# Local attention and channel mix: narrow products from unit 5, a halved first magnitude, new orders

## The chip, the cores and the metric

The kernel runs on one core of a Trainium2 chip. The metric is the device time of one execution in microseconds; the kernel before took 376.92 us (median of three runs, 376.2 to 378.92).

## What is computed

Sequences of 768 tokens, 4 of them, 8 heads of 64. Queries in chunks of 32 see 16 keys to the left, their own 32, 8 to the right and 8 memory keys: 64 keys, where the sequence has them all. The result, token by token 512 wide, goes through a channel mix with the token before it.

```python
def _attn_ref(q, k, v, mem_k, mem_v):
    ...
    for c in range(nc):
        ...
        k_full = np.concatenate([mem_k, k_ctx], axis=2)
        v_full = np.concatenate([mem_v, v_ctx], axis=2)
        scores = scale * np.matmul(q_c, k_full.transpose(0, 1, 3, 2))
        scores = scores - np.max(scores, axis=-1, keepdims=True)
        a = np.exp(scores)
        a = a / (np.sum(a, axis=-1, keepdims=True) + 1e-09)
        out[:, :, c_start:c_end] = np.matmul(a, v_full)

def _moe_ref(x, mu_k, mu_r, w_k, w_v, w_r):
    x_prev = np.concatenate([np.zeros((B, 1, D), dtype=np.float32), x[:, :-1, :]], axis=1)
    xk = mu_k * x + (1.0 - mu_k) * x_prev
    xr = mu_r * x + (1.0 - mu_r) * x_prev
    k = np.maximum(xk @ w_k, 0.0)
    v = k * k @ w_v
    r = 1.0 / (1.0 + np.exp(-(xr @ w_r)))
    return (r * v).astype(np.float32)
```

## The kernel before

The 3072 tokens are 12 **units** of 256 tokens, each of two **tiles** of 128. For each unit TensorE does, in this order of dependence:

- `s`, the scores (tile names s, PSUM, L572), from which VectorE takes the maximum (mx, L585) and subtracts it (L590), ScalarE the exponential (L596), VectorE the sum (L600) and the normalisation (L606). The PSUM buffer of the scores is one, and a narrow product (below) uses the same;
- from unit 3 on (MOVED) a transpose of e by VectorE (eT, L880), written to DRAM (eD) and read back as aTz by four transfers (L891); for units 0 to 2 four TensorE transposes for each tile (`t`, pt, L731), copied to aTz by ScalarE or VectorE (L390);
- `a`, the attention product px from aTz and the values vw. It has two forms. The **wide** one (L751, units 0 to 5) is sixteen 64x2x32 matmuls for each tile and gives the product already turned (64 passes for both tiles); ScalarE copies it to xT. The **narrow** one (L823, from unit ROWX = 6 on) is 64 small matmuls for both tiles (128 passes in the trace); a VectorE transpose of the result (L830) goes to DRAM (xD, L836) and returns as xT by four transfers (L841);
- the token mix (df L957 or L969, then xf, and xr as df, L989 and L991), split in a high part (xh) and a low part (xl, L1012);
- `h0` to `h3`, the projections with w_k (ph, L1459), then the squared relu (kf, ah, al) on ScalarE and VectorE; `g0` and `g1`, the gates with w_r (pr, L1348) of the unit after; `p1` to `p7`, seven Strassen-like products with w_v (accx, accy, accz, L1250), from which VectorE builds the output o (L1289, L1292, L1315 to L1322).

Unit 0 works in whole fp32 (ph L1405, pr L1339, pv L1548), unit 1 in split parts without the Strassen form (ph L1434, pv L1561). Products in split parts take three passes: high by high, low by high, high by low.

A weight chunk of 1 MB is loaded to raw (L438 for w_k, L440 for w_r and w_v), its magnitude is taken by ScalarE (w from raw, L456), its low bits by VectorE (L459), and both are joined by VectorE (L463). w0 to w3 are chunks of w_k, w4 and w5 of w_r, w6 to w9 of w_v; v2 and v3 are the values of tiles 2 and 3, q0a to q5 the queries and keys of units.

The order of TensorE is written by hand: LEAD for units 0 and 1, then STAGES, one line for each unit u, whose names mean: h, p and g as above (g of unit u+1), s the scores of unit u+2 and z those of u+3, a and b the products of the two tiles of unit u+1, x the product of unit u+2. A stage that is not listed takes line 0. LOADS orders the loads of SyncE's queue. The class Plan sets the orders of VectorE, ScalarE and the other transfers: it places each operation by a cost in us, by its due time and by what it depends on, and reckons with pauses in TensorE's instruction fetch (`fetched`). At the start some dependences are added by hand, so that the first unit's work goes in a set order (`prior`). While TensorE waits for its first operands it runs warm-up matmuls on zeros (warm, L1619), whose number is reckoned from the planned waiting time; an instruction of 512 columns is two passes in the trace.

## Time and profile before

| | before |
|---|---|
| timed runs | 376.92 us (376.2 to 378.92) |
| profiled execution | 378.26 us |
| its span | 376.4 us |
| TensorE busy | 369.4 us, 98% |
| TensorE's weight loads | 340.4 us, 90% |
| VectorE busy | 319.4 us, 85% |
| ScalarE busy | 211.1 us, 56% |
| chain that ended last | TensorE 80%, VectorE 13%, transfers 3%, ScalarE 2% |

The share of busy time of an engine tells how full it is on average; the view of waits tells what it stood idle for, and the chain of work follows the end back to its beginning. A matmul's row gives a start and a modelled end, and the next one starts before that end; so what one costs is read from start to start. A row of the timeline with x64 is a run of 64 matmuls of one kind, with the time from the first's start to the last's end. Bracketed at a row's end stands how long the engine was idle ahead of it, and what ended that.

### The profile page before, as it was taken

The numbers are of one execution on the slowest core, as the hardware profiler recorded it, in microseconds if no ns is written. First come the engines' busy times: TensorE is split into PE (matmuls) and PEld (weight loads), VectorE is DVE, ScalarE is ACT, GpSimd is POOL, SyncE is SP. The second block draws the span as 40 slices with busy tenths as digits, with TensorE's granted clock in tenths as the row PEclk, the third lists the DMA queues.
The fourth block names the chain that finished last, engine by engine and source line by source line (L and its number), as shares of the span: only waits on it lengthen the run. The fifth ranks groups of instructions, "written<-read, shape, count | busy, mean of one in ns | idle before, by whom it ended". The sixth has DMA issues, their size and how long they took to land.

```text
span 376.4 us, 11488 instructions
## 1 busy us (share of the span) xinstructions
PE 369.4 (98%) x5086; PEld 340.4 (90%) x5086; DVE 319.4 (85%) x518; ACT 211.1 (56%) x311; POOL 2.4 (1%) x9
## 2 busy tenths in 40 slices
PE   8999999999899999999999999999999999999996
PEld 6786579888899999999999999899999999999996
DVE  3898999899989599889878969998998997779274
ACT  2787897874585287355256447449339254154350
POOL 2000000000000000000000000000000000000000
PEclk9999999999999999999999999999999999999999
DMA  8999963222831743664693276186343431200101
GB/s 311 419 406 407 367 238 128 70 84 103 276 117 57 231 165 113 241 208 173 250 307 117 77 241 246 71 264 227 113 171 115 159 121 63 81 29 0 57 1 57
DMA packets 24146, 64.78 MB, mean 172 GB/s; under 512 B 2720, under 2 KB 10784, under 8 KB 23712
## 3 DMA queue, kind: packets, MB, share of 16 engines
q1 hardware_dynamic: 24096, 64.04, 47.9%
q8 instruction: 40, 0.66, 0.7%
q14 instruction: 10, 0.08, 0.1%
HBM read 49.88 MB, written 14.16 MB: 170 GB/s over the span
## 4 chain that ended last, share of the span: by engine, by line
PE 80%; DVE 13%; DMA 3%; ACT 2%; issue 1%; SPq 0%; DVEq 0%
PE ph L1459 25%; PE pr L1348 11%; PE accy L1250 10%; PE accx L1250 7%; PE accz L1250 6%; PE s L572 4%; PE pv L1561 3%; PE ph L1434 3%; PE px L751 3%; PE ph L1405 3%; PE warm L1619 2%; PE pv L1548 2%; PE px L823 2%; DVE al L1195 2%; DMA xT<-xD 1%
## 5 line engine op out<-in xcount | busy, mean ns | idle before, releaser
L1459 PE MATMUL ph<-xh,wk 128*128 128x256 f32 x320 | 89.0, 278 | 0.0
L1459 PE MATMUL ph<-xl,wk 128*128 128x256 f32 x320 | 88.0, 275 | 0.0
L1459 PE MATMUL ph<-xh,wl 128*128 128x256 f32 x320 | 88.0, 275 | 0.0
L1478 ACT ACTIVATE kf<-ph 128x512 f32<-128x512 f32 x46 | 27.0, 598 | 88.6 <-PE ph L1459 78.4
L1459 PEld LDWEIGHTS ph<-xh,wk 128*128 128x128 f32 x320 | 61.4, 192 | 0.8
L1459 PEld LDWEIGHTS ph<-xh,wl 128*128 128x128 f32 x320 | 61.4, 192 | 0.0
L1459 PEld LDWEIGHTS ph<-xl,wk 128*128 128x128 f32 x320 | 61.4, 192 | 0.0
L390 ACT CAST ah<-kf 128x512 fp32r<-128x512 f32 x47 | 28.7, 622 | 17.1 <-DVE kf L1173 11.6
L1195 DVE TENSOR_TENSOR al<-kf,ah 128x512 fp32r<-128x512 f32 x50 | 33.9, 683 | 2.5 <-ACT ah L390 2.2
L1348 PE MATMUL pr<-wr,xh 128*128 128x512 f32 x88 | 33.6, 382 | 0.0
L1348 PE MATMUL pr<-wl,xh 128*128 128x512 f32 x88 | 33.4, 379 | 0.0
L1348 PE MATMUL pr<-wr,xl 128*128 128x512 f32 x88 | 33.4, 379 | 0.0
L1485 ACT ACTIVATE kf<-kf 128x512 f32<-128x512 f32 x45 | 28.0, 633 | 1.0
L1250 PE MATMUL accx<-wv,ah 128*128 128x256 f32 x80 | 22.4, 280 | 0.0
L1250 PE MATMUL accx<-wl,ah 128*128 128x256 f32 x80 | 22.0, 275 | 0.4 <-issue 0.4
L1250 PE MATMUL accx<-wv,al 128*128 128x256 f32 x80 | 22.0, 275 | 0.0
L596 ACT ACTIVATE e<-e 128x1024 f32<-128x1024 f32 (+1 forms) x12 | 12.3, 1027 | 12.5 <-DVE e L590 12.5
L1357 ACT ACTIVATE sg_sb<-pr 128x512 f32<-128x512 f32 x24 | 14.0, 598 | 9.4 <-PE pr L1348 9.2
L1348 PEld LDWEIGHTS pr<-wr,xl 128*128 128x128 f32 x88 | 16.6, 189 | 2.3
L1348 PEld LDWEIGHTS pr<-wr,xh 128*128 128x128 f32 x88 | 16.7, 190 | 2.0
L1348 PEld LDWEIGHTS pr<-wl,xh 128*128 128x128 f32 x88 | 16.7, 190 | 1.8
L572 PEld LDWEIGHTS s<-qk 64*32 64x32 f32 x1472 | 15.4, 105 | 3.2 <-issue 2.2
(165 smaller groups left out, 964.3 us busy)
## 6 DMA issues: line engine op xcount, KB each, us to landing
qk<-in_qk_dram SPq DMA_DIRECT2D x23, 768.0 KB, 5.8
vw<-in_vw_dram SPq DMA_DIRECT2D x24, 512.0 KB, 5.2
out_dram<-o SPq DMA_DIRECT2D x23, 256.0 KB, 3.0
eD<-eT SPq DMA_DIRECT2D x9, 512.0 KB, 3.0
aTz<-eD SPq DMA_DIRECT2D x36, 128.0 KB, 3.1
raw<-in_w_v_dram SPq DMA_DIRECT2D x4, 1024.0 KB, 10.2
raw<-in_w_k_dram SPq DMA_DIRECT2D x3, 1024.0 KB, 13.0
xD<-aTz SPq DMA_DIRECT2D x6, 512.0 KB, 2.6
```

The costliest lines, as they stand in the source:

```text
L390: e.copy(dst, src)
L572: nc.tensor.matmul(s5[CHUNK * j : CHUNK * (j + 1), h, d - c, r, :], *operands(ts[d], r, j, slice(64 * h, 64 * h + 64)), start=True, stop=True,
L596: nc.scalar.activation(e, e, AF.Exp, scale=SCALE)
L751: nc.tensor.matmul(p3[64 * h : 64 * h + 64, 2 * g : 2 * g + 2, CHUNK * j : CHUNK * j + CHUNK], v[:, g, h, j, :], a[:, h, g, j, :], start=True,
L1195: nc.vector.tensor_sub(low(n), place[n](), T["ah", u, n].bitcast(F32))
L1250: nc.tensor.matmul(o, x, w, start=(n in fresh and c + i == 0), stop=(c == cs[-1] and i == 2), skip_group_check=True)
L1348: nc.tensor.matmul(pairs(p), x[:, place_of(u)[k], c * P : (c + 1) * P], woven(w), start=(k + n == 0), stop=(k == KT - 1 and n == 2),)
L1357: nc.scalar.activation(sg, p, AF.Sigmoid)
L1405: nc.tensor.matmul(p[:, i * UTOK + c * P : i * UTOK + (c + n) * P], T["w", id(wk_hl[0]), k][:, fc], T["xf", u, 0][:, k, z], start=(i + k + ...
L1459: nc.tensor.matmul(pairs(p[:, i * UTOK : (i + 1) * UTOK]), w[:, fc], x[:, :, place_of(u)[k]].rearrange("p t n -> p n t"), start=(k + n == ...
L1478: e.activation(part(), p, AF.Relu)
L1485: e.activation(q, q, AF.Square)
```

## The change

- ROWX falls from 6 to 5: unit 5's product takes the narrow form.
- The magnitude of w0 is taken in two halves of 128x512 (HALF). The sum of the first unit's first tile is done in two parts, the first of them as soon as its exponential is there.
- Of the dependences added by hand at the start two go (FORCE "nec" names those that stay): the copies of tile 1's transposes need no longer be ScalarE's, and w0's magnitude need no longer follow tile 0's copies.
- LOADS: w6, the first chunk of w_v, goes behind w7 and w8, and q5 ahead of q4.
- LEAD and the STAGES of units 2, 3, 4, 5, 9, 10, 11 and of line 0 are new.
- The planner's reckoning of fetch pauses, three of its costs and slacks, and the divisor by which the first group of warm-up matmuls is counted are changed; the first group has three instructions instead of four, the others as many as before.

```diff
-LOADS = "q0a q0b q1 id w0 v0 v1 w1a q2 w1b w2 w3 w4 q3 w5 w6 v2 w7 w8 w9 v3 q4 q5"
-LEAD = "s0.0.0 s0.0.1 s0.1 t0 t1 a0 a1 h0.0.0 h0.0.1 s1.0 h0.1.0 h0.2.0 h0.3.0 s1.1 h0.3.1 h0.3.2 h0.3.3 g0.0.0 g0.1.0 g0.0.1 t2 g0.1.1 t3 a2 v0.0.0 a3 v0.1.0 s2.0 v0.1.1 h1.0.0 h1.0.1 h1.0.2 v0.0.1 h1.0.3 h1.1.0 h1.1.1 h1.1.2 t4 t5 h1.1.3 a4 v1.0.0 a5 g1.0 g1.1 v1.0.1 s3.0 g2.0 v1.1.0 g2.1 v1.1.1"
+FORCE = "nec"
+HALF = 2
+LOADS = "q0a q0b q1 id w0 v0 v1 w1a q2 w1b w2 w3 w4 q3 w5 w7 w8 w6 v2 w9 v3 q5 q4"
+LEAD = "s0.0.0 s0.0.1 s0.1 t0 t1 a0 a1 h0.0.0 h0.0.1 s1.0 h0.1.0 h0.2.0 h0.3.0 s1.1 h0.3.1 g0.0.0 g0.1.0 h0.3.2 g0.0.1 h0.3.3 t2 t3 g0.1.1 a2 v0.0.0 a3 v0.1.0 s2.0 v0.1.1 v0.0.1 h1.0.0 h1.0.1 h1.0.2 h1.0.3 h1.1.0 h1.1.1 s3.0 t4 h1.1.2 h1.1.3 t5 v1.0.0 a4 a5 g1.0 v1.0.1 g1.1 v1.1.0 g2.0 g2.1 v1.1.1"
...
-    0: "z h0 h1 h2 h3 x p1 g0 p6 p7 g1 p5 p2 p4 p3",
-    2: "s h0 h1 a b h3 h2 p1 p7 g0 p6 g1 p5 p2 p3 p4",
+    0: "h0 h1 h2 z h3 p1 x g0 p6 p7 g1 p4 p5 p2 p3",
+    2: "h0 h1 s h2 a b h3 p1 p7 g0 p2 p6 g1 p5 z p3 p4",
...
-ROWX = 6
+ROWX = 5
...
-        def f_abs(z):
-            if z == 0:
+        def f_abs(z, n=1, h=0):
+            if z + h == 0:
                 T["w", id(hi), k] = sb(f"w{i}", [P, 2 * DM], f"w{i}")
-            m = T["w", id(hi), k][:, cols(z)]
-            nc.scalar.activation(m, word(1, F32, z), AF.Prelu, scale=TINY, alpha=-(2.0**32))
+            c = cols(z)
+            m = (c.stop - c.start) // n
+            m = slice(h * m, (h + 1) * m)
+            nc.scalar.activation(
+                T["w", id(hi), k][:, cols(z)][:, m], word(1, F32, z)[:, m], AF.Prelu, scale=TINY, alpha=-(2.0**32)
+            )
...
-        by = [("act", 0.5)] if t == 1 else either(act=(0.5,), dve=(0.61,))
+        by = [("act", 0.5)] if t == 1 and "t" in FORCE else either(act=(0.5,), dve=(0.61,))
...
-        if t == 0:
+        if t == 0 and "c" in FORCE:
             prior["abs"].deps += [c0, c1]
...
-                n = 0 if ("ph", 0, 0) in T else int((o.start - busy - 0.2) / (0.43 if busy else 0.86))
+                n = 0 if ("ph", 0, 0) in T else int((o.start - busy - 0.2) / (0.43 if busy else 1.1))
```

The orders of the two programs, first ScalarE's queue at the start, from the exponential of the first unit on (aTz are the turned probabilities, w from raw the magnitude of w0, xf the token mix). Before:

```order
L596 ACTIVATE e_137<-e_137 128x2x256
L390 COPY aTz<-pt_205 64x512 x2
L456 ACTIVATE w_229<-raw_187 128x1024
L390 COPY aTz<-pt_220 64x512 x2
L930 ACTIVATE xf_0_251<-px_234,mu_sb 128x128
L390 COPY xT_254<-px_234 128x4x128
L456 ACTIVATE w_274<-raw_198 128x512
```

In the changed kernel, from the same place:

```order
L613 ACTIVATE e_136<-e_136 128x2x256
L466 ACTIVATE w_208<-raw_187 128x512
L398 COPY aTz<-pt_199 64x512 x2
L466 ACTIVATE w_208<-raw_187 128x512
L398 COPY aTz<-pt_222 64x512
L951 ACTIVATE xf_0_251<-px_234,mu_sb 128x128
L398 COPY xT_255<-px_234 128x4x128
```

One half of the magnitude moved ahead of the first copies, the other stays between the copies, and of the second tile's two copies one has left this queue (it stands in VectorE's).

Then VectorE's queue around unit 3's transpose of e (mx, e, sum and eT belong to unit 3; `w` from `w` are sums of weight chunks, xl low parts of the mix). Before:

```order
L1058 TENSOR_TENSOR w_464<-w_496,w_464 128x4x128
L581 MEMSET s_0_994 32x2x4x16
L585 TENSOR_REDUCE mx_0_1063<-s_0_994 128x16
L590 TENSOR_TENSOR e_1080<-s_0_994,mx_0_1063 128x1024
L1012 TENSOR_TENSOR xl_0_1083<-df_945,xh_0_989 128x1024
L1058 TENSOR_TENSOR w_472<-w_526,w_472 128x4x128
L1058 TENSOR_TENSOR w_496<-w_496,w_464 128x4x128
L600 TENSOR_REDUCE sum_0_1087<-e_1080 128x16
L601 TENSOR_SCALAR sum_0_1087<-sum_0_1087 128x16
L602 RECIPROCAL sum_0_1087<-sum_0_1087 128x16
L606 TENSOR_TENSOR e_1080<-e_1080,sum_0_1087 128x1024
L880 STREAM_TRANSPOSE eT_1132<-e_1080 128x1024
```

In the changed kernel:

```order
L607 TENSOR_TENSOR e_1035<-s_0_807,mx_0_997 128x1024
L1607 TENSOR_TENSOR o_0_1037<-pv_0_932,sg_sb 128x512
L1012 SCALAR_TENSOR_TENSOR df_1015<-df_1015,mu_sb,xT_974 128x256 x4
L400 CAST xh_1_1060<-xf_1017 128x1024
L1033 TENSOR_TENSOR xl_1_1062<-xf_1017,xh_1_1060 128x1024
L617 TENSOR_REDUCE sum_0_1091<-e_1035 128x16
L618 TENSOR_SCALAR sum_0_1091<-sum_0_1091 128x16
L619 RECIPROCAL sum_0_1091<-sum_0_1091 128x16
L1033 TENSOR_TENSOR xl_0_1095<-df_1015,xh_0_1058 128x1024
L623 TENSOR_TENSOR e_1035<-e_1035,sum_0_1091 128x1024
L901 STREAM_TRANSPOSE eT_1112<-e_1035 128x1024
L1079 TENSOR_TENSOR w_487<-w_487 128x4x128
```

The sums of weight chunks that stood between the scores and the transpose of e now stand behind it, and a cast of xh with its low part xl_1 stands between.

Last TensorE's queue at unit 5's product. Before, it stands between two groups of projections:

```order
L1459 MATMUL ph_0_2068<-xh_0_1942,wk_71 128x256
L1459 MATMUL ph_0_2068<-xl_0_2015,wk_71 128x256
L1459 MATMUL ph_0_2068<-xh_0_1942,wl_735 128x256
L751 MATMUL px_2101<-aTz,vw_1725 64x2x32 x16
L751 MATMUL px_2124<-aTz,vw_1750 64x2x32 x16
L1459 MATMUL ph_1_2145<-xh_0_1942,wk_68 128x256
L1459 MATMUL ph_1_2145<-xl_0_2015,wk_68 128x256
```

In the changed kernel it stands between two of the seven products with w_v, one stage earlier:

```order
L1271 MATMUL accz_1946<-wv_73,ah_3_1831 128x256
L1271 MATMUL accz_1946<-wl_756,ah_3_1831 128x256
L1271 MATMUL accz_1946<-wv_73,al_3_1822 128x256
L844 MATMUL px_1974<-vw_1730,aTz 32x64 x32
L844 MATMUL px_1974<-vw_1757,aTz 32x64 x32
L1271 MATMUL accy_2046<-mh_1205,ah_3_1926 128x256
L1271 MATMUL accy_2046<-tl,ah_3_1926 128x256
```

The form changed from two groups of sixteen 64x2x32 matmuls to two rows of thirty-two 32x64 ones, whose operands change places, and the place moved from stage 4 into stage 3.

## Rows read from the trace of the kernel before

**Rows 1.** The page: busy times; then granted clock and GB/s in 40 slices.

```profile
PE 369.4 (98%) x5086; PEld 340.4 (90%) x5086; DVE 319.4 (85%) x518; ACT 211.1 (56%) x311; POOL 2.4 (1%) x9
...
PEclk9999999999999999999999999999999999999999
...
GB/s 311 419 406 407 367 238 128 70 84 103 276 117 57 231 165 113 241 208 173 250 307 117 77 241 246 71 264 227 113 171 115 159 121 63 81 29 0 57 1 57
```

**Rows 2.** TensorE's waits: line, releaser, then us, times, longest.

```profile
PE px L751 <- DMA aTz<-eD: 1.0, 1, 1.0
PE px L751 <- ACT aTz L390: 0.7, 1, 0.7
PE accy L1250 <- DVE o L1292: 0.5, 1, 0.5
PE accx L1250 <- issue: 0.4, 1, 0.4
```

**Rows 3.** TensorE's timeline, first 17 us: start, length, what [idle before it].

```profile
1.18 3.78 PE L1619 MATMUL warm<-zero_sb 128*128 128x256 f32 x8 [1.18 <-DVE zero_sb L380]
4.89 1.19 PE L654 MATMUL s<-qk 64*32 64x48 f32 x64
...
8.57 2.42 PE L1619 MATMUL warm<-zero_sb 128*128 128x256 f32 x10
...
15.23 1.15 PE L751 MATMUL px<-aTz,vw 128*64 128x64 f32 x32 [0.67 <-ACT aTz L390]
16.31 0.94 PE L1405 MATMUL ph<-xf,w 128*128 128x128 f32 x6
```

**Rows 4.** ScalarE's timeline from 9 to 17 us.

```profile
11.58 1.17 ACT L390 COPY aTz<-pt 64x512 f32<-64x512 f32 x2 [0.70 <-PE pt L731]
12.78 1.20 ACT L456 ACTIVATE w<-raw 128x1024 f32<-128x1024 f32 x1
...
16.55 0.69 ACT L456 ACTIVATE w<-raw 128x512 f32<-128x512 f32 x1
```

**Rows 5.** The chain that ended last, from 80 to 104 us: start, length, what.

```profile
81.55 1.43 PE s L572 x89
...
87.22 1.20 DVE w L1058 x2
...
97.03 4.44 DMA aTz<-eD
...
101.51 2.09 PE px L751 x64
```

**Rows 6.** TensorE's timeline around unit 5's product.

```profile
157.05 2.08 PE L751 MATMUL px<-aTz,vw 128*64 128x64 f32 x64
159.06 0.38 PE L1459 MATMUL ph<-xh,wk 128*128 128x256 f32 x1
159.28 0.28 PE L1459 MATMUL ph<-xl,wk 128*128 128x256 f32 x1
```

**Rows 7.** TensorE's timeline around unit 6's product.

```profile
176.85 1.48 PE L823 MATMUL px<-vw,aTz 64*32 64x64 f32 x128
178.27 0.38 PE L1250 MATMUL accy<-t1h,ah 128*128 128x256 f32 x1
```

**Rows 8.** VectorE's timeline, one row.

```profile
223.39 1.21 DVE L957 TENSOR_TENSOR df<-xT 128x1008 f32<-128x1008 f32 x1 [3.25 <-DMA xT<-xD]
```

**Rows 9.** The loads of w_v: issue, landing, ScalarE, VectorE and the first reader.

```profile
25.50 9.37 SPq L440 DMA_DIRECT2D raw<-in_w_v_dram  x3
...
raw<-in_w_v_dram SPq DMA_DIRECT2D x4, 1024.0 KB, 10.2
...
36.41 1.16 ACT L456 ACTIVATE w<-raw 128x1024 f32<-128x1024 f32 x1 [0.71 <-DMA raw<-in_w_v_dram]
...
38.48 2.35 DVE L463 SCALAR_TENSOR_TENSOR w<-w,raw 128x1024 uint32<-128x1024 uint32 x2
...
41.84 1.13 PE L1548 MATMUL pv<-w,kf 128*128 128x512 f32 x2
```

## Prediction before the changed kernel was run

> **What bounds the kernel now.** I read the page first, then TensorE's waits, then the chains of the places where it waits. The page's line of busy times says that TensorE works 369.4 us of the 376.4 us span, 98%, while VectorE stands at 85% and ScalarE at 56% [rows 1]. So only two things can shorten the kernel: less work in TensorE's queue, or fewer of its gaps, and there are few of those. The view of TensorE's waits lists what is left to take [rows 2]: an attention product that waited 1.0 us for a transfer (aTz<-eD), one that waited 0.7 us for ScalarE's copies at the start, a partial sum that waited 0.5 us for VectorE, and 0.4 us that the view puts to "issue". With the stretch before the first projection (ph at 16.31 us, [rows 3]) this is all that a new order could win; the rest is matmuls that stand in both kernels.
>
> **The start.** TensorE's timeline shows eight passes of the warm-up matmul, then the first scores at 4.89, and so on to the last attention product at 15.23 and the first ph at 16.31 [rows 3]. Eight passes are four instructions; of the changed program's order the first group has three. They took 3.78 us, 0.47 a pass, so two passes less put the first scores 0.94 us earlier, if their operands are there; the other warm-up groups have the same counts as before. Further down it is ScalarE that decides: its row shows copies at 11.58, then the 1.20 us magnitude of the first weight chunk at 12.78, then the other tile's copies [rows 4], and the product at 15.23 waits for those copies by the view of waits (0.7, [rows 2]). ScalarE had been idle 0.70 us ahead of 11.58. Half a magnitude is the 128x512 form, 0.69 us [rows 4]. Cut in two, the first half fits into that idle 0.70, and one of the later two copies may go to VectorE; what stays between the copies is 0.69 instead of 1.20. That is 0.51 us on the path if all else stays, and the earlier scores add something unless VectorE, serial here, holds them. The cost of the cut is one more instruction, 2 x 0.69 - 1.20 = 0.18 us, which lies in ScalarE's idle time. I take -0.55. Bounds: -0.75 (the whole 0.7 wait, and a little of the 0.94), and +0.3 if the scores run at the slow pass for longer (below).
>
> The passes of the first group take 0.47 us, those of the third 0.24 [rows 3]: the array works at half its pace at first and at its full one later, though the page's line of the granted clock reads nine tenths or more, the 2.4 GHz level, in every slice [rows 1]. The Trainium skill, "TensorE: Matmul & The Clock Gate", section "What's actually happening", says that the throttled state is the default and activity releases it; that would speak against a warm-up matmul less, and the rows agree with the two paces but show no run with another count.
>
> **Unit 5's product, narrow instead of wide.** The wide pair of unit 5 starts at 157.05 and the projection behind it at 159.06: 2.01 us [rows 6]. The narrow form that unit 6 on already uses starts at 176.85 and is followed at 178.27: 1.42 us [rows 7]. Difference -0.59; I take -0.60. Its price lies elsewhere: one VectorE transpose of 1.2 us and a round trip through DRAM of the product. The row of VectorE shows what such a trip can cost: it sat idle 3.25 us until the last xT transfer landed at 223.39 [rows 8]. The product of unit 5 stands a stage ahead of its use, so I count 0 for the trip, and VectorE, busy 85% of the span [rows 1], carries 1.2 us more. If the cover is gone, the mix of unit 5 is late by up to 3 us, and the projections of unit 5 behind it: that would turn the -0.6 into a loss of 2.4.
>
> The narrow form is 64 instructions, 128 passes in the row, in 1.42 us: 22 ns from one instruction to the next [rows 7]. The Trainium skill, "TensorE: Matmul & The Clock Gate", section "Wait — 56ns, not 53.3ns?", says that this distance never falls below about 25 ns however small the matmul; by that (an estimate) the product takes 1.6 us if an instruction is meant, a term of -0.4, and 3.2 us if a pass is, a loss of 1.2. The row shows the very operation at 1.42, below both, so the sum goes by it.
>
> **The order of TensorE.** A small product between projections costs a pass twice its size behind it: the next ph starts 0.22 us after the one that follows the product, where 0.11 is the pitch of a 128x256 pass [rows 6]; the same 0.1 is lost ahead of it. So each place where the array goes from projections to small products and back costs some 0.2 us. I counted these places in both orders: 27 before, 26 in the changed one. Term: -0.2.
>
> **Unit 3's scores earlier.** The largest gap ends at 101.51 (1.0 us, and some 0.1 around it). Its chain reads backwards from the product at 101.51 to the transfer that ran from 97.03 for 4.44 us, past VectorE's sums of weight chunks at 87.22, and to unit 3's scores at 81.55 [rows 5]. From scores to product these are 20 us. The changed order puts these scores behind h1.1.1, ahead of two quarters of a projection, two tiles' transposes and products, two gates and two parts of v1 that stood before them, while the product stays near its place. It is VectorE's queue that passes the gain on. Before, five sums of weight chunks stand ahead of the transpose of e, 0.6 each (two take 1.20, [rows 5]); in the changed order none does, and two casts come in that another engine did before. I reckon these at 0.7 each, as the 128x512 pass of ScalarE (an estimate, from [rows 4]). So the transpose comes 3.0 - 1.4 = 1.6 us earlier, and 1.0 suffices. Term: -1.1 (the wait and the 0.1). Bounds: 0, if VectorE takes its maximum and subtraction no earlier than now, and -1.1. The scores share one PSUM buffer, so those of the next unit wait for their subtraction; that is ready long before.
>
> **The loads.** The first chunk of w_v goes from the first place among its four loads to the third. The issue row of the three later ones starts at 25.50 and ends 9.37 later [rows 9], so the last is issued near 34.5. The second landed at 36.41, since ScalarE waited for it till then; the transfers move some 407 GB/s in that slice [rows 1], 2.6 us for 1 MB. So what comes third lands between 36.4 and 39.0; I take 37.7. Then 1.16 for its magnitude and 1.18 for its join (half of 2.35) [rows 9]: ready at 40.0, at worst 41.3. Its first reader, v0.0.0, starts at 41.84 now, and 0.75 earlier with the start and the switch saved: 41.1. So 0 to 0.2 us of wait. The values of the second tile (v2) land 1.3 us behind, 39.0 (up to 40.3), and the product that reads them is half a wide pair ahead of v0.0.0, at 40.1. I take +0.1 for both.
>
> **Other waits.** Against the sum for accy (VectorE's o, [rows 2]) and the 0.4 of issue the new orders of six stages may do anything: those gaps go or others come. VectorE's queue in the third stage is the tightest place, since unit 3's softmax and mix fall together there with a product's conversions. The nearest rows are the present gaps, 0.5 and 0.4 [rows 2]. I take 0: as much comes as goes. Bounds: -1.0 (none comes) and +1.5 (three more of 0.5).
>
> **The sum.** -0.55 - 0.60 - 0.20 - 1.10 + 0.10 + 0 = -2.35 us. The profiled run took 378.26 us (span 376.4), so 375.9 in its own terms; it stands 1.3 us above the median of the three timed runs, 376.92 (376.2 to 378.92). From the median: 374.6 us, 0.6% less.
>
> **Rivals.**
> - *Everything comes.* Start -0.75, product -0.6, switch -0.2, unit 3's wait -1.1, and both small waits gone, -1.0: -3.65, 373.3 us; with a little more from the scores' 0.94, 1%. For it: each part has its row, and the gaps do not depend on each other. Against: six stages get new orders, and no row shows that these leave no gap.
> - *The waits form again.* Unit 5's conversions and unit 3's softmax meet on VectorE, and +1.5 stands where 0 was: 376.1 us, a gain of 0.2%. For it: VectorE at 85%. Against: it has 57 us idle in all.
> - *The first w_v chunk comes late* (the other side). If its buffer comes free only when the last chunk's does now, it is issued at 34.5, and lands by the median of 10.2 us [rows 9] at 44.7; ready 47.0, 5.9 us behind 41.1, and nothing of the other chunk is ready to fill it: 380.4 us. A landing by 38.8 costs nothing; from 41.2 on, 2.4 us later, the whole gain is eaten and the kernel is slower than before. For it: the row of 9.37 us for three issues is mostly waiting. Against: of these three only the last waits long, if the second was issued near the first, as its landing at 36.41, 10.9 us after 25.50, says.
> - *The array speeds up later*, with a warm-up matmul less: the scores and the warm passes up to 8.57 then run at 0.47 instead of 0.24, at most 0.9 us on the path: 375.5 us.
> - *The narrow product is slow here*, 3.2 us, if each of its passes keeps a distance of its own: +1.8 on the sum, 376.4 us. Unit 6's row of 1.42 speaks against it. (This is what the page's rule above would do.)
>
> **How the numbers follow.** My forecast (between -1.5 and -3.2 us) has 0.54, everything 0.17, waits formed again 0.17, the late chunk 0.08, the late clock 0.03, the slow narrow product 0.01. The range leaves out 2 in 10: below, everything by 0.9 us of the runs' own scatter (376.92 - 376.2 = 0.7, and 0.2 of the scores), 372.4; above, the waits formed again by +1.5 of the scatter (half of the 2.0 between median and highest, and 0.5), 377.6. A measurement of this kernel can tell about 1%, 3.8 us, from no change. Faster by more than that is only the case in which everything comes: 0.17. Slower by more needs 380.7, half of the late chunk's chance: 0.04. The rest, 0.79, lies within 1%.
>
> **What would show it.** In the changed kernel's timeline the first ph should start near 15.75; the list of TensorE's waits should have no px for aTz<-eD near 100; the product of unit 5 should be a row of about 1.42 us; v0.0.0 should follow the product ahead of it without idle time. The prediction is wrong if TensorE's idle time after the first ph is above 3 us or below 1, or if the first ph starts after 16.3.

## The result: 379.6 us against 377.4, and the profile after

Eight executions of the changed kernel have a median of 379.58 us (377.83 to 381.51), eight of the kernel before on the same chip 377.37 us (376.2 to 378.92). The ratio is 1.0065, with a 95% interval of 1.0037 to 1.0092: slower by 0.65%, where 0.6% less was forecast. The profiled execution took 379.40 us, its span is 377.6.

The page of the changed kernel, in four of its lines: the span, the busy times (they answer [rows 1]), the granted clock in 40 slices, and the transfers of instructions in queue q8 with packets, MB and share.

```profile
span 377.6 us, 11611 instructions
...
PE 369.3 (98%) x5148; PEld 339.9 (90%) x5148; DVE 323.0 (86%) x522; ACT 206.6 (55%) x309; POOL 2.4 (1%) x9
...
PEclk9999999999999999999999998999999999999999
...
q8 instruction: 40, 0.66, 0.7%
```

TensorE is as busy as before, 369.3 us, in a span that is 1.2 us longer. One slice of the clock, the 25th, is below nine tenths. TensorE's waits (line, releaser, then us, times, longest; they answer [rows 2]):

```profile
PE px L844 <- issue: 2.0, 1, 2.0
...
PE px L772 <- ACT aTz L398: 0.6, 2, 0.3
PE px L844 <- PE accx L1271: 0.5, 1, 0.5
PE s L671 <- DMA qk<-in_qk_dram: 0.3, 1, 0.3
...
PE px L844 <- DMA aTz<-eD: 0.2, 1, 0.2
```

Unit 3's wait for aTz<-eD of 1.0 us, that for VectorE's o and the 0.4 of "issue" at accx are gone from this list, as hoped. In their place one product, the narrow one of unit 8, has 2.0 us of "issue" in it and 0.5 us ahead of it. TensorE's timeline there (start, length, what, [idle before it]):

```profile
225.19 0.28 PE L1271 MATMUL accx<-wv,al 128*128 128x256 f32 x1
225.95 1.43 PE L844 MATMUL px<-vw,aTz 64*32 64x64 f32 x110 [0.49 <-PE accx L1271]
229.42 0.41 PE L844 MATMUL px<-vw,aTz 64*32 64x64 f32 x18 [2.03 <-issue]
...
230.39 0.63 PE L1369 MATMUL pr<-wr,xl 128*128 128x512 f32 x1
230.82 0.63 PE L1369 MATMUL pr<-wr,xh 128*128 128x512 f32 x1
...
233.92 0.38 PE L1369 MATMUL pr<-wr,xl 128*128 128x512 f32 x1
```

The product starts at 225.95, runs 110 of its 128 passes, and stands still until 229.42 with nothing to wait for: in the trace none of its instructions between 226.05 and 229.42 waits for a semaphore. Behind it the gate's passes start 0.43 us apart (230.39, 230.82) where 0.22 is the rule. The windows around the pause (us, then busy time of PE, PEld, DVE, ACT, POOL with counts, granted clock, DMA share, GB/s) show why:

```profile
226.20:226.90 0.70, 0.70 (x86) 0.70 (x83) 0.70 (x2) 0.56 (x2) 0.00 (x0) 1.00 0.00 0
229.90:231.90 2.00, 2.00 (x6) 1.62 (x7) 2.00 (x2) 1.98 (x2) 0.00 (x0) 0.57 0.56 158
231.90:233.40 1.50, 1.50 (x5) 1.14 (x5) 0.34 (x1) 0.00 (x0) 0.00 (x0) 0.50 0.91 358
```

The granted clock is 1.00 in the product and 0.57 and then 0.50 behind the pause, which is the 1.2 GHz level; the trace's record of the clock has it from 230.18 to 233.60.

The 0.5 us ahead of the product are another thing. The view puts them to accx, whose last matmul had ended at 225.47, but the product writes to the PSUM buffer of the scores, and VectorE's subtraction, which empties this buffer of unit 9's scores, ends at 225.85, 0.10 us before the product starts:

```profile
224.63 1.22 DVE L607 TENSOR_TENSOR e<-s,mx 128x1024 f32<-128x1024 f32 x1
```

The start came out better than forecast in this execution. Its timeline (answers [rows 3]):

```profile
1.18 2.93 PE L1640 MATMUL warm<-zero_sb 128*128 128x256 f32 x6 [1.18 <-DVE zero_sb L388]
4.04 0.68 PE L671 MATMUL s<-qk 64*32 64x48 f32 x32
4.99 0.46 PE L671 MATMUL s<-qk 64*32 64x48 f32 x32 [0.27 <-DMA qk<-in_qk_dram]
5.38 1.56 PE L1640 MATMUL warm<-zero_sb 128*128 128x256 f32 x6
...
13.93 1.15 PE L772 MATMUL px<-aTz,vw 128*64 128x64 f32 x32 [0.31 <-ACT aTz L398]
15.02 2.05 PE L1426 MATMUL ph<-xf,w 128*128 128x128 f32 x16
```

The first ph starts at 15.02, 1.29 us earlier than before. TensorE's last matmul, however, starts at 374.25, where before it was at 372.94. So the way from the first ph to the last matmul, which I call **the stretch** from here on, went from 356.6 to 359.2 us: +2.6, where the sum had -1.8.

### The profile page after: what moved, and what is told of

The parts are those of the page before. It is cut to its first block, busy times and chain, and to the rows that moved or that the text cites. A ratio compares the mean times of both kernels' runs of the same rounds, so it can differ in the third digit from the quotient of the medians.

```text
span 377.6 us, 11611 instructions
## 1 busy us (share of the span) xinstructions
PE 369.3 (98%) x5148; PEld 339.9 (90%) x5148; DVE 323.0 (86%) x522; ACT 206.6 (55%) x309; POOL 2.4 (1%) x9
## 4 chain that ended last, share of the span: by engine, by line
PE 77%; DVE 9%; DMA 9%; ACT 2%; issue 1%; SPq 1%; DVEq 0%
PE ph L1480 25%; PE pr L1369 14%; PE accy L1271 10%; PE accx L1271 6%; PE accz L1271 6%; DMA sg_sb<-in_w_r_dram 4%; PE pv L1582 4%; PE s L589 3%; PE ph L1455 3%; PE px L844 3%; DMA eD<-eT 2%; PE pv L1569 2%; DMA raw<-in_w_k_dram 2%; PE px L772 1%; DVE w L475 1%
## 5 line engine op out<-in xcount | busy, mean ns | idle before, releaser
L1499 ACT ACTIVATE kf<-ph 128x512 f32<-128x512 f32 x47 | 27.8, 597 | 92.4 <-PE ph L1480 91.7
L398 ACT CAST ah<-kf 128x512 fp32r<-128x512 f32 x49 | 29.6, 620 | 16.6 <-DVE kf L1194 13.9
L1369 PE MATMUL pr<-wr,xh 128*128 128x512 f32 x88 | 34.4, 391 | 0.0
L1369 PE MATMUL pr<-wr,xl 128*128 128x512 f32 x88 | 34.2, 389 | 0.0
L1506 ACT ACTIVATE kf<-kf 128x512 f32<-128x512 f32 x47 | 29.3, 631 | 2.4 <-DVE kf L1501 1.2
L1369 PEld LDWEIGHTS pr<-wr,xh 128*128 128x128 f32 x88 | 17.1, 194 | 2.4
L1369 PEld LDWEIGHTS pr<-wl,xh 128*128 128x128 f32 x88 | 17.1, 194 | 2.1
L589 PEld LDWEIGHTS s<-qk 64*32 64x32 f32 x1472 | 15.3, 105 | 2.7 <-issue 1.5
L589 PE MATMUL s<-qk 64*32 64x64 f32 x1472 | 17.4, 225 | 0.0
```

Of the source, the lines that this page charges most:

```text
L398: e.copy(dst, src)
L589: nc.tensor.matmul(s5[CHUNK * j : CHUNK * (j + 1), h, d - c, r, :], *operands(ts[d], r, j, slice(64 * h, 64 * h + 64)), start=True, stop=True,
L1369: nc.tensor.matmul(pairs(p), x[:, place_of(u)[k], c * P : (c + 1) * P], woven(w), start=(k + n == 0), stop=(k == KT - 1 and n == 2),)
L1499: e.activation(part(), p, AF.Relu)
L1506: e.activation(q, q, AF.Square)
```

## The experiments

The question was what the pause inside unit 8's product is, since it and what lies around it hold more than the whole loss: 0.5 us of wait ahead of it, 2.25 of pause and 1.7 of half pace make 4.5 us. (A pause is counted here from one matmul's start to the next one's; the idle time in brackets, from the modelled end, is 0.2 to 0.4 us less.) The experiments come in the order in which they were run. All ratios are to the kernel before, run beside them; "stretch" is read from each trace as above.

**One stage's order put back.**

```diff
+    6: "z h0 h1 h2 h3 x p1 g0 p6 p7 g1 p5 p2 p4 p3",
```

> The changed kernel with one stage's order put back: in stage 6 the scores of unit 9 stand ahead of h0 and unit 8's narrow product behind h3, as before. Theory F (in the changed kernel's stage 6 the scores and the narrow product, 256 PE records each, stand so close together, around a 1.5 MB load of queries, that the instruction fetch comes late inside the product: 2.0 us of 'issue' at 227.4, and then about 1.6 us in which the granted clock is at its lower level): no pause over 0.7 us in stage 6, no lower clock, TensorE's last matmul 3.5 to 4.5 us earlier than in the changed kernel, time near 375.2 (379.6 - 4.4). Rival P (the pause belongs to the place in the program, not to that order): a pause of about 2 us stays near 227 or comes in the next stage, time within 1 us of the changed kernel's.

Measured: 383.93 us, ratio 1.0174 (1.0104 to 1.0244). The pause is there, and longer: the product starts at 224.66 and stands still 2.6 us (2.41 idle) ahead of its last six passes. Another product waits 4.7 us at 261.92, 0.10 us behind the end of VectorE's subtraction at 261.82: the queues were laid out anew, and it waited for the scores' buffer. Theory F as I had put it (too little distance between scores and product) falls: with four groups of projections between them the pause stays. The number of TensorE's instructions ahead of the product is nearly the same in both orders, and this is what led further.

**The product one gate later.**

```diff
+    6: "h0 h1 h2 z h3 p1 g0 x p6 p7 g1 p4 p5 p2 p3",
```

> The changed kernel with unit 8's narrow product one gate later in stage 6 (behind g0 instead of ahead of it), 2.6 us further from unit 9's scores. Theory F: the fetch has 2.6 us more, so the pause of 2.0 us inside the product falls below 0.5 us and the clock stays at its upper level; the 0.5 us wait ahead of the product (for the scores' PSUM buffer) goes too; time near 375.2. Rival P: the pause stays at 1.5 us or more. A cost on the other side: the product's transfers come 2.6 us later, which may show as idle time of VectorE ahead of df, up to 1 us on TensorE.

Measured: 379.21 us, ratio 1.0047 (1.0016 to 1.0078), where 375.2 was forecast. The pause is down to 0.8 us (0.59 idle, where less than 0.5 was forecast), and no lower clock follows it; but the planner laid out other queues anew, and a product a stage earlier waits 2.35 us at 205.16, which takes the gain. The view puts this wait to "issue"; the rows of VectorE and TensorE show that it is the scores' buffer again, since the subtraction ends at 205.06:

```profile
203.84 1.22 DVE L608 TENSOR_TENSOR e<-s,mx 128x1024 f32<-128x1024 f32 x1
205.16 1.14 PE L845 MATMUL px<-vw,aTz 64*32 64x64 f32 x56 [2.35 <-issue]
```

**The loads of queries moved away.**

```diff
+        moved = [o for o in ops if getattr(o, "tile", 0) in (20, 21)]
+        queue = [o for o in ops if o.eng == "dma"]
+        goal = queue[queue.index(moved[-1]) + 7]
+        ops = [o for o in ops if o not in moved]
+        i = ops.index(goal) + 1
+        ops[i:i] = moved
```

> The changed kernel with only one thing moved: the two loads of unit 10's queries and keys (768 KB each), issued at 220.7, are issued behind unit 8's xT transfers (about 238). All engines' orders are the same otherwise. Theory F1 (the instruction fetch was late because it stood behind these loads, which filled the DMA engines from 223 to 226): the pause inside unit 8's product shrinks from 2.0 us to under 0.7 us, no lower clock, time near 375.8. Rival F2 (the fetch is late because 256 records of the product go through in 1.4 us, whatever the DMA engines do): the pause stays at 1.7 to 2.3 us and the time within 1 us of the changed kernel's. Between: about 1 us.

Measured: 379.79 us, ratio 1.006 (1.0035 to 1.0085), as the changed kernel. TensorE's timeline at the product:

```profile
228.37 1.43 PE L845 MATMUL px<-vw,aTz 64*32 64x64 f32 x110 [0.50 <-PE accx L1272]
231.84 0.41 PE L845 MATMUL px<-vw,aTz 64*32 64x64 f32 x18 [2.03 <-issue]
```

The pause has 2.03 us of idle time again and comes behind the 110th pass again, though the DMA engines were idle while the product ran (a share of 0.00 from 228.4 to 229.4). F1 falls: these loads are not the cause.

**The start alone.** The tables of before, with the start of the changed kernel:

```diff
-ROWX = 5
+ROWX = 6
...
```

> The changed kernel with the tables of before put back (order of the loads, LEAD, all STAGES, ROWX = 6), so that of the change only the start (halved magnitude, split sum, the two dependences less, a warm-up instruction less) and the planner's reckoning stay. Theory: the start alone gives 1.2 us, so the first ph begins at 15.0 to 15.2 and the time is 1.0 to 1.5 us under that of before (about 376.0 against 377.4). Rival: the start's gain is given back at the next wait (loads that come no earlier than before hold the first unit's chunks): the first ph at 15.1, but less than 0.4 us left at the end.

Measured: 382.58 us, ratio 1.0131 (1.0084 to 1.0178), stretch 362.6. It does not answer its question: the changed planner lays the old tables out worse (unit 3's product waits 2.5 us at 103.95 for aTz<-eD), and the first ph was at 17.08 though its program at the start is the same. That made the start itself a question.

**What the traces had in common.** Each q8 transfer of the page brings 0.66 MB / 40 = 16.5 KB (16,384 bytes in the trace), and the 10,296 matmuls and weight loads of the changed kernel make 257 for each. So I counted TensorE's instructions (matmuls, weight loads and semaphore instructions of the trace) up to each pause that no operand and no buffer explains:

```
kernel                       record at which it pauses   record mod 256   from the transfer's start to the end of the pause
before                       5824                        192              2.57 us
changed                      6848                        192              2.41 us
one stage's order put back   6848                        192              2.42 us
product one gate later       6848                        192              2.20 us
loads moved away             3776, 6848                  192              2.43, 2.42 us
start alone                  5824, 8128                  192              2.18, 2.36 us
```

The pauses stand 256 records apart or a multiple of it, and end 2.2 to 2.6 us after a q8 transfer begins. If that is the cause, a pause must move when instructions are put ahead of everything, whatever the order behind them.

**56 records more, order unchanged.** The 14 warm-up matmuls cut in two (the same for four in the two runs behind it). Each of them has 256 columns, not the 512 that the section on the kernel before gives, and leaves two weight loads and two matmuls in the trace, so each cut adds four records:

```diff
+PIECES = [2] * 14
...
+                    n = 2 * P // PIECES[0]
+                    for x in range(PIECES.pop(0)):
+                        nc.tensor.matmul(warm[:, x * n : (x + 1) * n], zero_sb[:, :P], zero_sb[:, x * n : (x + 1) * n], start=True, stop=True)
```

> The changed kernel with each of the 14 warm-up matmuls of 256 columns cut into two of 128: the same work and the same orders of all engines, but 56 PE records more ahead of everything. In all traces so far pauses inside a stream of PE instructions stand at record 256k+192 of the trace, and end 2.4 us after an instruction transfer begins. Theory A (the pause of 2.2 us inside unit 8's product, and the lower clock behind it, come from where the boundary of a 256-instruction block falls): with the boundary 56 records earlier in the program, the block that ends inside the product has some 3 us of slow projections in it; the pause at the product's 110th matmul goes or falls under 0.8 us, no pr at half pace behind it, and the stretch from the first ph to the last matmul shrinks from 359.2 us to about 355 to 356.5. A pause may come up at another burst, at record 256k+192 again. Rival B (the product waits for data in its middle): the pause stays at the 110th matmul, 2.0 to 2.4 us.

Measured: 381.64 us, ratio 1.0126 (1.0108 to 1.0144). Unit 8's product runs through. Pauses stand at records 3264, 5056 and 7872, all 192 mod 256, the last two in the middle of projections and of a gate that run behind narrow bursts:

```profile
168.27 0.28 PE L1481 MATMUL ph<-xl,wk 128*128 128x256 f32 x1
170.38 0.27 PE L1481 MATMUL ph<-xh,wl 128*128 128x256 f32 x1 [1.83 <-issue]
...
258.75 0.38 PE L1370 MATMUL pr<-wr,xl 128*128 128x512 f32 x1
260.98 0.38 PE L1370 MATMUL pr<-wr,xh 128*128 128x512 f32 x1 [1.85 <-issue]
```

Theory A holds for where the pause is, and B falls. Its size I had wrong: the stretch is 359.3, since 0.6 + 2.1 + 2.2 us of pauses came in the place of the one, where 355 to 356.5 was forecast. The clock stayed at 1.00 in this trace.

**112 and 168 records more.**

> As the run before, but 112 PE records more (seven warm-up matmuls cut in four, seven in two). Theory A: the pause is not at the 110th matmul of unit 8's product; where pauses inside a stream are, they stand at record 256k+192; the stretch from first ph to last matmul is 354.5 to 357.5, by the luck of the other bursts. Rival B: the same pause at the same place as in the changed kernel, stretch near 359.

> As the two runs before, but 168 PE records more (all warm-up matmuls cut in four). Theory A: as for 112 records; boundaries fall 168 records earlier in the program, so bursts that were safe may be hit and the reverse; pauses only at record 256k+192. Rival B: unchanged pause.

Measured: 397.87 and 400.5 us, ratios 1.0548 (1.0503 to 1.0592) and 1.062 (1.0605 to 1.0636). Most of that is the start: in these two the first ph comes at 25.6 and 33.1 us, because passes of 64 columns start 0.213 us apart like those of 128, and the pace is slow through most of the head (in the second, four transposes at 28.5 take 1.06 us where 0.60 is the rule). Behind it the pauses are at records 4288, 5056, 7872 and at 4288, 8896, once more all 192 mod 256, between 1.2 and 4.2 us long, and unit 8's product runs through in both (having waited 0.5 and 1.0 us for the scores' buffer). So theory A holds for the place. Its stretch for the first of the two, 354.5 to 357.5, missed: it is 365.1 us, with three pauses of 1.6 to 3.2 us and two spells at the lower clock; in the second it is 362.1.

**Four warm-up instructions.**

```diff
-                n = 0 if ("ph", 0, 0) in T else int((o.start - busy - 0.2) / (0.43 if busy else 1.1))
+                n = 0 if ("ph", 0, 0) in T else int((o.start - busy - 0.2) / (0.43 if busy else 0.86))
```

> The changed kernel with four instructions instead of three in the first warm-up group, as before. In five traces of kernels with three the first ph starts at 15.0, 15.2, 16.3, 17.0 and 17.1 us, since the warm-up and score passes change from 0.47 to 0.24 us at anything from 5.9 to 9.9 us; PE idles 0.2 to 0.3 us ahead of the second half of the first scores. Theory W (the missing warm-up matmul leaves that idle time, and the pace then sometimes rises later): with four the idle time is gone, the pace changes by 7 us and the first ph starts at 15.3 to 15.9 here. Rival V (the moment varies from run to run with three or four): the pace changes at 8 us or later in this run too, or the idle time is gone without effect. The rest as in the changed kernel, with the pause in unit 8's product (four records' shift).

Measured: 379.35 us, ratio 1.0049 (1.0014 to 1.0084), with the pause at record 6848. The idle time ahead of the second half of the scores is gone, the trace's record of the faster clock begins at 7.40, and the first ph is at 16.23. Theory W's time for it was too early by 0.3, but its main point (the faster pace comes near 7 us) is borne out. The median is the same as with three.

**The gate ahead of the product, nothing else.** If the block that ends inside the product had more slow work in it, the transfer would be there in time. One swap of two neighbours in TensorE's order, all other queues kept:

```diff
+        gate = [o for o in ops if o.eng == "pe" and o.rank == due["g", 7, 0]]
+        product = [o for o in ops if o.eng == "pe" and o.rank == due["a", 16]]
+        ops = [o for o in ops if o not in gate]
+        i = ops.index(product[0])
+        ops[i:i] = gate
```

> The changed kernel with one swap in TensorE's order: in stage 6 the gate g0 stands ahead of unit 8's narrow product instead of behind it; the orders of all other engines are the same. Theory A (instruction blocks of 256 records): the block in which the product ends now has 24 slow gate records more ahead of it, so the pause inside the product falls from 2.25 us to 0.5 to 1.0 us; the wait of 0.6 us for the scores' buffer ahead of it goes; no pr runs at half pace behind it (1.6 us). The stretch from first ph to last matmul falls from 359.2 us to 355.2 to 356.0, the time to 375.5 to 376.5, against 377.4 before. Rival D (the gain is given back because the product, 2.6 us later, delays unit 8's mix): stretch 357.5 or more, with idle time of TensorE behind VectorE's df of unit 8.

Measured: 375.72 us (374.39 to 376.74, 12 runs), ratio 0.9936 (0.9914 to 0.9959). The whole list of TensorE's waits in this kernel, and its timeline at the product:

```profile
PE warm L1646 <- DVE zero_sb L388: 1.2, 1, 1.2
PE px L772 <- ACT aTz L398: 0.6, 2, 0.3
PE s L671 <- DMA qk<-in_qk_dram: 0.3, 1, 0.3
PE ph L1426 <- DVE xf L959: 0.2, 1, 0.2
```

```profile
229.10 0.38 PE L1369 MATMUL pr<-wr,xl 128*128 128x512 f32 x1
229.41 1.48 PE L844 MATMUL px<-vw,aTz 64*32 64x64 f32 x128
230.82 0.38 PE L1271 MATMUL accy<-mh,ah 128*128 128x256 f32 x1
```

The product follows the gate without a pause and takes 1.41 us; there is no "issue" left. The trace shows how close this is. The transfer that brings the next block begins at 227.72, now 1.69 us ahead of the product and not 1.05 behind its start, and record 6848 is reached at 230.35, 2.63 us after the transfer began; the pauses end 2.2 to 2.6 us after one. The wait for the scores' buffer is gone too, since the subtraction had ended at 227.28. The stretch is 354.0 us, 5.2 less than in the changed kernel: more than forecast, since even the 0.5 to 1.0 us that I had left for the pause are gone. Theory A is shown by this and by the shifts together; D falls.

**The same with four warm-up instructions.**

> The run before with four instructions in the first warm-up group instead of three. Theory W (with three the pace rises at 5.9 to 9.9 us, with four at about 7): the first ph at 16.0 to 16.5, where kernels with three have 15.0 to 17.1; the median within 0.6 us of the run before, with less scatter. If the late rise hurts most executions with three, this one is 0.5 us faster.

Measured: 375.08 us (374.75 to 375.8, 7 runs), ratio 0.993 (0.9901 to 0.9959). This is the lowest median of the study, 2.5 us under the kernel before. The scatter is smaller than in the run before, as forecast (1.05 us from lowest to highest against 2.35); the 0.64 us between the two medians are not clear of that scatter. TensorE's timeline at the start, of the run before and of this one:

```profile
5.64 2.93 PE L1646 MATMUL warm<-zero_sb 128*128 128x256 f32 x6
...
17.08 1.60 PE L1426 MATMUL ph<-xf,w 128*128 128x128 f32 x12
```

```profile
6.01 2.24 PE L1646 MATMUL warm<-zero_sb 128*128 128x256 f32 x6
...
16.22 1.94 PE L1426 MATMUL ph<-xf,w 128*128 128x128 f32 x15
```

With three, the six passes of the second warm-up group took 2.93 us here, 0.49 each, all at the slow pace, and the first ph came at 17.08; in the changed kernel's own trace they took 1.56 us and the first ph came at 15.02. With four, the group took 2.24.

**The kernel before, with 60 records more, and once more as it is.** The first cuts its 15 warm-up matmuls in two, as above.

> The kernel before with its 15 warm-up matmuls cut in two halves of 128 columns, which puts 60 PE records ahead of everything and leaves all orders as they are. Theory A (before stood well by where its instruction blocks end): pauses come up at record 256k+192 in other places than at 199.6 us, the stretch from first ph to last matmul grows from 356.6 to 358 to 361 us, and the time by 1 to 4 us. Rival (bursts before are spaced so that the alignment matters little): stretch within 0.7 us of 356.6.

> The kernel before, unchanged, profiled a second time, to see what of its start and its pauses repeats. Theory W: the pace of the warm-up passes rises near 6.6 us again and the first ph starts at 16.2 to 16.5; the pause near 199.6 (record 5824) is there with 0.5 to 0.7 us. Rival V: the pace rises at another time and the first ph moves by more than 0.5 us.

Measured: with 60 records more 380.66 us, ratio 1.0072 (1.0036 to 1.0107); once more 377.2 us, ratio 0.9992 (0.9967 to 1.0018). TensorE's timeline of the first at its longest pause, and the windows behind it:

```profile
195.65 0.38 PE L1461 MATMUL ph<-xh,wk 128*128 128x256 f32 x1
198.66 0.37 PE L1461 MATMUL ph<-xl,wk 128*128 128x256 f32 x1 [2.63 <-issue]
```

```profile
200.00:202.00 2.00, 2.00 (x12) 2.00 (x12) 0.00 (x0) 0.00 (x0) 0.00 (x0) 0.54 0.63 258
202.00:204.00 2.00, 2.00 (x21) 2.00 (x20) 1.06 (x2) 0.34 (x1) 0.00 (x0) 1.00 0.05 16
```

Sixty records of nothing make the kernel before 3.5 us longer in its stretch (360.1 against 356.6), with pauses at records 5824 and 6336 of 2.9 and 1.5 us and the clock at 0.54 behind the first. So the orders of before were good for their own place of the block boundaries, and worse for the one other place that was tried. Unchanged, it pauses at record 5824 again, 0.63 us. In that second profile unit 3's product has no wait for aTz<-eD:

```profile
100.40 0.28 PE L1459 MATMUL ph<-xh,wl 128*128 128x256 f32 x1
100.61 1.61 PE L751 MATMUL px<-aTz,vw 128*64 128x64 f32 x47
```

It follows the projections after 0.21 us, where the first profile had the 1.0 us of [rows 2, 5]. The stretch is 355.2 instead of 356.6, and the first ph is at 16.50 instead of 16.31.

## Why the prediction was wrong, point by point

- **Other waits: the step that failed.** The sum let the small gaps come and go at 0, with bounds of three gaps of 0.5 us, because the nearest rows were 0.5 and 0.4 [rows 2]. But the 0.4 of "issue" was a pause of another kind, an instruction block that came late, and what such a pause costs elsewhere cannot be read from its row. In the three traces with the changed kernel's order at this place (changed, loads moved away, four warm-up instructions) the transfer begins 1.05 to 1.10 us after the product and the pause ends 2.4 us later, so 3.5 us in all, while the product reaches the boundary after 1.25: 2.25 us of pause. Behind it came what no row of before showed, the lower clock: the gate's twelve passes start from 229.75 to 233.92, in 4.17 us, where the same passes behind the same product took 2.47 in the run with 56 records (229.72 to 232.19), so 1.7 us. Together with the 0.5 of the scores' buffer ahead of the product this is 4.5 us where the sum had 0 and the upper bound 1.5. The diff itself said what to look at: it changes the planner's reckoning of these pauses, in which the number 256 stands (FETCH). I counted its edits at nothing.
- **Unit 5's narrow product.** It saves the 0.6 us when nothing holds it (1.41 us for unit 8's above, so the rival of 3.2 us falls). But it has 256 records, where the wide one has 128, so it also moves every block boundary behind it by half a block against the program. That price was left out. In the changed kernel's own trace it also waits 0.23 us for its transfer:

```profile
143.20 0.30 PE L844 MATMUL px<-vw,aTz 64*32 64x64 f32 x2
143.72 1.46 PE L844 MATMUL px<-vw,aTz 64*32 64x64 f32 x126 [0.23 <-DMA aTz<-eD]
145.10 0.38 PE L1271 MATMUL accy<-mh,ah 128*128 128x256 f32 x1
```

  From 143.20 to 145.10 are 1.90 us, so of the 0.6 only 0.1 was left there.
- **The start.** Right in kind and mis-sized both ways (its bounds were -0.75 and +0.3). The half magnitude and the earlier scores work: the first ph came at 15.02 where the faster pace came early, 1.3 us before and not 0.55, since VectorE's chain followed the scores (its first maximum is at 4.79 instead of 5.64). The scores came 0.85 us earlier, not 0.94: a slow warm-up pass starts 0.427 us after the one before it, and the 0.47 was the row's length divided by eight. But with three warm-up instructions TensorE idles 0.2 to 0.3 us ahead of the second half of the scores (4.99 above), and the pace changes at different times: in seven traces with three the first ph is at 15.0, 15.2, 15.3, 16.3, 17.0, 17.1 and 17.1 (the runs of 64-column pieces left out), in five with four at 16.2 to 16.6. The traces' records of the granted clock begin only with this change, which is why the page reads nine tenths in its first slice too; they begin at 4.90, 5.45, 5.86, 7.34, 9.64, 10.30 and 10.45 with three, and at 6.61 to 7.40 with four. The rival "the array speeds up later" had 0.03 and a price of 0.9; it is what happens in four of these seven, and the latest is 2.1 us behind the earliest. The middle one, 16.3, is where the kernel before has it (16.31 and 16.50), so the term was worth nothing in the middle. Whether the idle time, the missing matmul or mere scatter from one execution to the next does this, no run separates.
- **Unit 3's scores earlier.** It did what was said: VectorE's transpose begins at 87.99 instead of 91.34 (1.3 us of this came with the start, so 2.1 where 1.6 was reckoned), and the product follows the projections without waiting. The reckoning itself was off: of the five sums of weight chunks that it counts ahead of the transpose, the trace of before has two (87.11 and 87.70) between these scores and the transpose; what moved is the scores, which start at 64.25 instead of 81.48.

```profile
87.99 1.25 DVE L901 STREAM_TRANSPOSE eT<-e 128x1024 f32<-128x1024 f32 x1
```

```profile
101.74 0.28 PE L1480 MATMUL ph<-xh,wl 128*128 128x256 f32 x1
101.94 1.27 PE L772 MATMUL px<-aTz,vw 128*64 128x64 f32 x36
```

  But the 1.1 us was the value of one execution; the second profile of before has none of this wait. The term was worth between 0 and 1.1.
- **The loads.** Right. ScalarE took the magnitude of w6 at 37.72, when it landed (37.7 was reckoned, the middle of 36.4 to 39.0, so to the second digit it is luck), VectorE joined it at 39.36, and v0.0.0 started at 41.08 behind its product with no idle time:

```profile
37.72 1.19 ACT L466 ACTIVATE w<-raw 128x1024 f32<-128x1024 f32 x1 [0.89 <-DMA raw<-in_w_v_dram]
...
39.36 1.23 DVE L475 SCALAR_TENSOR_TENSOR w<-w,raw 128x1024 uint32<-128x1024 uint32 x1
...
40.00 1.15 PE L772 MATMUL px<-aTz,vw 128*64 128x64 f32 x32 [0.24 <-ACT aTz L398]
41.08 3.70 PE L1569 MATMUL pv<-w,kf 128*128 128x512 f32 x8
```

  The product at 40.00 lost 0.24, not to v2 but to ScalarE's copies of the turned probabilities. Of the 1.29 us that this execution had gained at the first ph, 0.76 were left here (41.08 against 41.84).
- **The switch of orders**, -0.2, and the wait for VectorE's o, which fell from 0.45 to 0.13: nothing speaks against them, and no run measures them by themselves. With the pause taken out by one swap the kernel's median is 375.72, 1.9 us under the kernel before beside it, and 375.08 with the fourth warm-up instruction, where the sum had -2.35. So the rest came out about right as a sum, and partly by luck: its stretch of 354.0 is 2.6 us under the first profile of before and 1.2 under the second, where the sum had 1.8, and of its parts the start and unit 5's product gave less in the traces than they were put at. The mechanism that decided was not in it.

The lower clock behind a pause is not certain: it came after 2.25 us (changed) and 2.9 us (before with 60 records), and not after pauses of 2.1 and 2.2 us in the run with 56 records, nor after the 2.6 us (2.41 idle) of the first experiment. It did not come in every execution of the changed kernel either: of the eight timed ones six have a mean granted clock of 0.991 to 0.996 and a median of 380.3 us, and two have 1.00 and 377.83 and 378.75 us; with the gate first all twelve have 1.00. This fits the parts: 375.72 with 0.5 and 2.25 added is 378.5 us, and with the 1.7 of half pace 380.2. The Trainium skill, "TensorE: Matmul & The Clock Gate", section "What's actually happening", says that the throttled state is the default and activity releases it. The traces agree as far as they go: between the first rise and the last matmul every spell at 0.50 begins in or soon behind an idle time of TensorE, and the 2.41 us of the first experiment have none behind them.

What stays open is what sets the moment at which the transfer of a block begins: at the twenty pauses TensorE stood anywhere from 4 to 256 records past the last boundary when it did, so the records at which a pause can fall are known ahead of a run, and whether it comes and how long it lasts are not.

## What to carry to other kernels

Where one engine's instruction stream is long and a burst of very short instructions runs through it (here 256 records in 1.4 us), find out at which instruction numbers it pauses without a wait, and how far apart these are: a change that only adds or removes instructions moves all of them, and can cost more than it saves. A neutral shift of the stream (a few harmless instructions at its head, few and cheap enough not to delay the head itself) tells in one run whether a kernel's time hangs on its alignment. And a wait of 1 us that is read from one execution should be seen in a second one before it goes into a sum.

## What the runs showed of the hardware that I had not expected

- Twenty pauses in twelve traces, all of those in the middle of a stream of one operation that the view puts to "issue", are at records that are 192 mod 256 of TensorE's count; a pause ends 2.2 to 2.6 us after a transfer of 16.5 KB in the instruction queue begins, whether the other transfers take 0.04 or 0.97 of the DMA engines' time. Three more waits that the view puts to "issue" (4.7, 2.35 and 1.0 us, at the first matmul of a narrow product) are elsewhere; all three end 0.10 us behind VectorE's subtraction of the scores.
- Passes of 64 and of 128 columns of the fp32 warm-up matmul both start 0.213 us apart at the slow pace, where those of 256 columns start 0.427 apart; and behind a head of only 64-column passes the slow pace was still there at the first products (64 passes of px in 3.7 us at 29.5, where 2.0 is the rule).
- With the same orders and the same program at its head, the moment of the faster pace moved the first projection between 15.0 and 17.1 us from one execution to another.
